# Hashed attention and SwiGLU on one core: two head pairs of batch 0 turned later, three casts of q on another engine, value means and weight loads at other slots

## The chip, the cores and the metric

The kernel runs on one core of a Trainium2 chip. The metric is the device time of one execution in microseconds, and lower is better. Three executions of the kernel before took 342.06, 342.91 and 343.15 us, so the median is 342.91 us.

## The reference

There are 4 batches with 8 heads each, 768 positions per head and 64 values per position. Attention is masked by a hash: a query sees a key only if the signs of their projections on 6 random directions agree. The result goes through an RMS norm and a SwiGLU block with 512 model columns and 1536 hidden columns.

```python
q_bits = (np.einsum('bhsd,dk->bhsk', q, proj) > 0).astype(np.int64)
k_bits = (np.einsum('bhsd,dk->bhsk', k, proj) > 0).astype(np.int64)
q_bucket = np.sum(q_bits * powers, axis=-1)
k_bucket = np.sum(k_bits * powers, axis=-1)
mask = q_bucket[:, :, :, None] == k_bucket[:, :, None, :]
scores = scale * np.matmul(q, k.transpose(0, 1, 3, 2))
scores = np.where(mask, scores, -1000000000.0)
scores = scores - np.max(scores, axis=-1, keepdims=True)
attn = np.exp(scores)
attn = attn / (np.sum(attn, axis=-1, keepdims=True) + 1e-09)
return np.matmul(attn, v).astype(np.float32)

rms = np.sqrt(np.mean(x * x, axis=-1, keepdims=True) + 1e-06)
xn = x / rms * rms_g
g = xn @ w_gate
silu = g * (1.0 / (1.0 + np.exp(-g)))
val = xn @ w_val
return (silu * val @ w_out).astype(np.float32)
```

## The kernel before

The work is cut into eight units `u`: four batches, each with two halves of 384 query rows. A unit has eight heads, and a head of a unit has three chunks of 256 keys. One chunk is one slot. `scores` makes two matmuls from the fp16 tile `QK` into `s_ps`, `probs` makes one exponential (L333) from it into `psb`, and `av` multiplies `psb` with the values `vl` into `o_ps`. The 6 signs of the hash are 6 more rows of `QK` (rows 64 to 69), so that the score matmul itself adds a large number where the buckets agree, and the exponential's bias takes it away. `cvb` holds a small multiple of the value means and is added to `o_ps` in `attn_out` (`otmp`, L360), then divided (`rcp`, `x`) and squared (`sq`) for the norm.

Heads come in pairs `hp`. A pair of batch 0 is brought into `QK` by these steps. `load_natural` loads q and k (tiles `qn`, `kn`), `load_v` the values (`vn`); all come from the queue of SyncE (SP) and take one of eight buffers of `lpool`, so a load waits for the last reader of its buffer. `turn_pe` turns one head on TensorE with three transposes into a PSUM bank (`t_ps`) and VectorE copies that into `qT` or `kT` (L150). `cast_pool` casts to fp16 into `QK` with two instructions on GpSimd (POOL), each for one half of the positions and both heads; a single such cast is `cast_part` (L164), which takes the engine as an argument. `hash_pair` makes 16 matmuls on `qT` and `kT` into two banks `d_ps` (L222), and `signs` turns these into `bits` on VectorE (L211). `send_pair` moves the bits into `QK` with four DMAs on SP (L261), in the order k and q of the first head, then k and q of the second; pair 1 moves one head with VectorE copies instead (L252). `v_prep` casts the values into `vl` (L290), and `v_mean` makes six matmuls (`m_ps`, L306) and writes `cvb` (L309). All these banks come from a pool of three.

The order is written out by hand. `at(w, s, f, ...)` puts a step into slot `24 * w + s`. In slot t the program first gives out `scores` of slot t+1, then `probs` of slot t, then the slot's steps, so each engine has its instructions in that order and keeps to it. Heads run as units 0 and 1 alternating for the first pair, then heads 2 to 7 of unit 0, then heads 2 to 7 of unit 1. So scores of batch 0's pair 1 are first made in slot 11 (for slot 12), those of pair 2 in slot 17 (for slot 18), and those of pair 3 in slot 23 (for slot 24). The last head of unit 0 has its `av` in slots 31 and 32, then follow its norm, `turn_x` in slot 37, and from slot 38 on the gate and value matmuls (`g_ps`, `v_ps`, L425) of unit 0, which need the weights `wg` and `wv`. These weights are loaded with a cast by the queue of POOL (`load_w`, L520), in halves of the hidden columns.

Batch 1's first two pairs are prepared in the same stretch: their loads stand in slots 8 and 17, their turns in slots 22 to 25 and 27 to 30. The norm's scale `rstd` is computed on POOL; the second weight halves stand behind it in POOL's order.

Of the kernel before, what the change touches and what calls it, by code (L numbers as in the profile page):

```python
# [33 lines left out]
def kernel(  # L34
# [12 lines left out]
    nc = tc.nc  # L47
# [485 lines left out]
    def at(w, s, f, *a):  # L533
        plan[NS * w + s].append(lambda: f(*a))
# [43 lines left out]
    at(0, 0, second_head)  # L578
    at(0, 1, cast_part, 0, 0, "q", 1)
    at(0, 1, v_prep, 0, 0)  # L580
    for hp, s0 in ((1, 2), (2, 5), (3, 11)):
        at(0, s0, new_pair, 0, hp)
        at(0, s0, turn_pe, 0, hp, 0, "k")
        at(0, s0 + 1, turn_pe, 0, hp, 1, "k")
        at(0, s0 + 1, cast_pool, 0, hp, "k")
        at(0, s0 + 2, turn_pe, 0, hp, 0, "q")
        at(0, s0 + 3, turn_pe, 0, hp, 1, "q")
        at(0, s0 + 3, cast_pool, 0, hp, "q")
        at(0, s0 + 4, hash_pair, 0, hp)
        if hp == 1:  # L590
            at(0, s0 + 5, send_pair, 0, hp, (1,))
            at(0, s0 + 5, move_head, 0, hp, 0)
        else:
            at(0, s0 + 5, send_pair, 0, hp)
# [4 lines left out]
    at(0, 8, v_prep, 0, 1, nc.vector)  # L599
    at(0, 13, v_prep, 0, 2, nc.vector)  # L600
    at(0, 19, v_prep, 0, 3, nc.vector)
    for hp, t in enumerate((4, 18, 24, 30)):
        at(0, t, v_mean, 0, hp, 2, range(6))
    for i, t in enumerate((20, 33)):
        cols = slice(i * DFF // 2, (i + 1) * DFF // 2)
        at(0, t, load_w, wg, moe_w_gate, 0, 4, cols)
        at(0, t + 3, load_w, wv, moe_w_val, 0, 4, cols)
        at(0, 39 + 3 * i, load_w, wo, moe_w_out, 6 * i, 6)
# [121 lines left out]
    def behind_norm(t):  # L730

        return t - t % NS + 7 if 2 <= t % NS < 7 else t

    for (b, hp), (load, kturns, qturns, _) in spots.items():
# [7 lines left out]
        t = behind_norm(qturns[-1] + 2)  # L742
# [66 lines left out]
```

## Time and profile before

| quantity | value |
|---|---|
| median of three executions | 342.91 us (342.06 to 343.15) |
| profiled execution, its own time | 340.8 us |
| its span, first to last instruction | 339.0 us |
| TensorE busy | 330.5 us, 97% |
| ScalarE busy, of it exponentials L333 | 224.6 us, 168.0 us |
| VectorE busy | 234.4 us |
| GpSimd busy | 151.2 us |
| granted TensorE clock, mean | 1.000 |
| first and 39th exponential start | 9.54 and 50.92 us |
| first gate matmul starts | 51.09 us |

The span is counted from the first to the last instruction, and 1.8 us of the execution's time lie around it. The list of costly groups is led by the exponentials (192 of 900 ns) and by the matmuls of scores, gate, value and projection. In the order of time, a row has the start in us, the length in us, the engine, the line, the operation, the tiles and how many instructions are merged; in brackets stands how long the engine was idle before it and what ended that. "SPq" rows are SyncE's DMA issues, and a row of several issues includes the time that the queue stood waiting between them.

### The profile page before, as it was taken

The page shows a single profiled execution, that of the slowest core. Times are in us where ns is not written, and L with a number is a line of the kernel's source. Part 1 is how long each engine was busy: PE and PEld are TensorE (multiplying, and loading weights), DVE is VectorE, ACT ScalarE, POOL GpSimd, SP SyncE. Part 2 cuts the span into 40 slices and gives each one's busy share as a digit, 9 for nine tenths or more (in the row PEclk, how much of TensorE's full clock was granted, in tenths as well). Part 3 has the DMA queues.
Part 4 walks back from the last instruction along what each step waited for, and adds up shares of the span by engine and source line. Part 5 has one row for each costly group of instructions (what it writes and reads, how often), then busy time and mean ns, then how long its engine had stood idle before and what let it go on. Part 6 is the DMA issues. An engine that isn't in the chain of part 4 may idle for free.

```text
span 339.0 us, 7797 instructions
## 1 busy us (share of the span) xinstructions
PE 330.5 (97%) x3004; PEld 197.4 (58%) x3004; DVE 234.4 (69%) x489; ACT 224.6 (66%) x325; POOL 151.2 (45%) x204
## 2 busy tenths in 40 slices
PE   7899899999999999999999999999999999999996
PEld 3565656655566556655656556555656656664554
DVE  3786696776879658884788658884776546674870
ACT  2878787676757767776677667776667767764322
POOL 3577848517463533747373523738281121112000
PEclk9999999999999999999999999999999999999999
DMA  7942989981809618070826118000200010001002
GB/s 243 316 144 22 262 135 209 221 154 36 190 19 164 118 65 169 8 141 6 163 76 96 51 65 167 9 1 7 95 3 3 2 62 34 0 2 64 32 0 93
DMA packets 79692, 30.92 MB, mean 91 GB/s; under 512 B 64988, under 2 KB 76712, under 8 KB 79656
## 3 DMA queue, kind: packets, MB, share of 16 engines
q1 hardware_dynamic: 75528, 25.45, 31.2%
q0 software_dynamic: 3680, 4.72, 8.4%
q8 instruction: 23, 0.38, 0.5%
q10 hardware_dynamic: 448, 0.27, 0.2%
q14 instruction: 13, 0.11, 0.1%
HBM read 28.32 MB, written 6.29 MB: 102 GB/s over the span
## 4 chain that ended last, share of the span: by engine, by line
PE 90%; DVE 4%; DMA 3%; ACT 2%; issue 1%; POOL 0%; DVEq 0%
PE v_ps L425 18%; PE g_ps L425 18%; PE y_ps L454 17%; PE s_ps L321 17%; PE o_ps L346 9%; PE d_ps L202 3%; DMA qn<-in_q_dram 3%; PE d_ps L222 2%; PE x_ps L408 2%; PE t_ps L148 2%; ACT psb L333 2%; PE z_ps L515 1%; PE y_ps L473 1%; DVE a L442 0%; PE m_ps L306 0%
## 5 line engine op out<-in xcount | busy, mean ns | idle before, releaser
L333 ACT ACTIVATE psb<-s_ps,ebias 128x768 f16<-128x768 f32 x192 | 168.0, 900 | 26.9 <-PE s_ps L321 25.9
L321 PE MATMUL s_ps<-QK 70*128 70x384 f16 x384 | 93.9, 326 | 1.8 <-ACT psb L333 1.1
L433 ACT ACTIVATE t<-g_ps 128x384 f32<-128x384 f32 x96 | 47.2, 491 | 56.1 <-PE g_ps L425 55.9
L425 PE MATMUL g_ps<-xnT,wg 128*128 128x384 f16 x384 | 82.5, 325 | 0.2
L425 PE MATMUL v_ps<-xnT,wv 128*128 128x384 f16 x384 | 81.7, 325 | 0.3 <-DVE a L442 0.2
L442 DVE SCALAR_TENSOR_TENSOR a<-t,g_ps 128x384 f32<-128x384 f32 x96 | 52.8, 550 | 28.2 <-ACT t L433 26.8
L454 PE MATMUL y_ps<-wo,ht 128*128 128x512 f16 x276 | 68.0, 378 | 0.0
L367 POOL TENSOR_TENSOR x<-otmp,rcp 128x384 f32<-128x384 f32 x31 | 25.7, 830 | 89.6 <-DVE rcp L365 89.3
L346 PEld LDWEIGHTS <-psb 128*128 128x128 f16 x1152 | 52.2, 97 | 15.8 <-issue 0.6
L443 DVE SCALAR_TENSOR_TENSOR ht<-a,v_ps 128x384 f16<-128x384 f32 x96 | 53.2, 554 | 11.7 <-PE v_ps L425 3.2
L346 PE MATMUL o_ps<-vl,psb 128*128 128x65 f16 x1152 | 56.3, 193 | 0.0
L321 PEld LDWEIGHTS <-QK 70*128 70x128 f16 x384 | 34.7, 98 | 35.5 <-issue 11.9
L425 PEld LDWEIGHTS <-wv 128*128 128x128 f16 x384 | 35.2, 97 | 22.6 <-issue 1.8
L425 PEld LDWEIGHTS <-wg 128*128 128x128 f16 x384 | 34.7, 97 | 21.2 <-DVE xnT L414 0.6
L454 PEld LDWEIGHTS <-ht 128*128 128x128 f16 x276 | 24.7, 97 | 22.7
L372 POOL TENSOR_TENSOR sq<-x 128x384 f32<-128x384 f32 x31 | 25.7, 828 | 2.4
L194 POOL CAST QK<-kT 64x768 f16<-64x768 f32 x20 | 16.4, 822 | 22.6 <-DVE kT L174 10.0
L466 ACT COPY ysb<-y_ps 128x512 f32<-128x512 f32 x23 | 13.5, 586 | 18.5 <-PE y_ps L454 18.5
L360 DVE TENSOR_TENSOR otmp<-o_ps,cvb 128x390 f32<-128x390 f32 x32 | 17.9, 559 | 10.3 <-PE o_ps L346 10.1
L194 POOL CAST QK<-qT 64x768 f16<-64x768 f32 x20 | 16.5, 827 | 18.4 <-DVE qT L181 17.0
L376 DVE TENSOR_REDUCE ssp<-sq 128x3 f32<-128x384 f32 x32 | 17.0, 530 | 10.0 <-POOL sq L372 10.0
L414 DVE TENSOR_TENSOR xnT<-x_ps,gcol 128x512 f16<-128x512 f16 x22 | 14.5, 685 | 5.8 <-PE x_ps L408 5.8
(70 smaller groups left out, 262.8 us busy)
## 6 DMA issues: line engine op xcount, KB each, us to landing
vn<-in_v_dram SPq DMA_DIRECT2D x16, 384.0 KB
out_dram<-ysb SPq DMA_DIRECT2D x23, 256.0 KB
qL<-in_q_dram SPq DMA_DIRECT2D x40, 96.0 KB
kL<-in_k_dram SPq DMA_DIRECT2D x40, 96.0 KB
kn<-in_k_dram SPq DMA_DIRECT2D x5, 384.0 KB
qn<-in_q_dram SPq DMA_DIRECT2D x5, 384.0 KB
wg<-in_moe_w_gate_dram POOLq DMA_DIRECT2D x2, 768.0 KB, 7.5
wv<-in_moe_w_val_dram POOLq DMA_DIRECT2D x2, 768.0 KB, 11.3
```

The source lines that it names most:

```text
L194: nc.gpsimd.tensor_copy(QK[b, 2 * hp + hh, "h"][0:64, o : o + S], src[64 * hh : 64 * hh + 64, :])
L321: nc.tensor.matmul(ps[:, j, 0:HALF], QK[b, h, "h"][0:KROWS, S + jt * 128 : S + (jt + 1) * 128], QK[b, h, "h"][0:KROWS, half * HALF : (half ...
L333: nc.scalar.activation(psb[u, h][:, 2 * ch : 2 * ch + 2, :], sps.pop((u, i))[:, :, 0:HALF], AF.Exp, bias=ebias, scale=ESCALE,)
L346: nc.tensor.matmul(o[:, c, hh, 0:65], psb[u, h][:, jt, c * 128 : (c + 1) * 128], vls[b % 2][:, h, 2 * (jt % 3) + jt // 3 if b in PARITY el ...
L360: nc.vector.tensor_add(tmp[:, :, :, 0:65], o[:, :, :, 0:65], cvb[b % 2][:, 2 * hp : 2 * hp + 2, 0:65].unsqueeze(1).to_broadcast([128, 3, 2 ...
L367: eng.tensor_mul(xd.rearrange("p c (h d) -> p c h d", h=2), tmp[:, :, :, 0:64], r.to_broadcast([128, 3, 2, 64]),)
L372: eng.tensor_mul(sq, xd, xd)
L425: nc.tensor.matmul(ps, w[:, kt, fs], xnT[u][:, kt, :], start=(kt == 0), stop=(kt == 3))
L433: nc.scalar.activation(t, fbank[u, ft, "g_ps"], AF.Tanh, scale=0.5)
L442: nc.vector.scalar_tensor_tensor(out=a, in0=t, scalar=1.0, in1=g, op0=ALU.add, op1=ALU.mult)
L443: nc.vector.scalar_tensor_tensor(out=ht[u][:, ft, :], in0=a, scalar=0.5, in1=vv, op0=ALU.mult, op1=ALU.mult)
L454: nc.tensor.matmul(y, ht[u][:, ft, c * 128 : (c + 1) * 128], wo[:, ft, :], start=(ft == 0), stop=(ft == NF - 1),)
```

## The change

Pairs 2 and 3 of batch 0 start their turns in slots 8 and 14, where they started in slots 5 and 11; casts, hash and sending of the bits keep their distance to that start, so pair 2's bits are sent in slot 13 and pair 3's in slot 19. For pairs 1, 2 and 3 the cast of q is split: its first half of the positions goes to VectorE, its second stays on POOL. Since pair 3's bits are now sent in slot 19, the loads of batch 1's pair 1, still in slot 17, stand ahead of them in SP's queue. The value means of pairs 1, 2 and 3 move from slots 18, 24 and 30 to slots 16, 21 and 31, and the weight halves of `wg` from slots 20 and 33 to 22 and 34; `wv` follows three slots behind each.

```diff
-    for hp, s0 in ((1, 2), (2, 5), (3, 11)):
+    for hp, s0 in ((1, 2), (2, 8), (3, 14)):
         at(0, s0, new_pair, 0, hp)
         at(0, s0, turn_pe, 0, hp, 0, "k")
         at(0, s0 + 1, turn_pe, 0, hp, 1, "k")
         at(0, s0 + 1, cast_pool, 0, hp, "k")
         at(0, s0 + 2, turn_pe, 0, hp, 0, "q")
         at(0, s0 + 3, turn_pe, 0, hp, 1, "q")
-        at(0, s0 + 3, cast_pool, 0, hp, "q")
+        at(0, s0 + 3, cast_part, 0, hp, "q", 0, 0, 2, nc.vector)
+        at(0, s0 + 3, cast_part, 0, hp, "q", 1)
         at(0, s0 + 4, hash_pair, 0, hp)
...
-    for hp, t in enumerate((4, 18, 24, 30)):
+    for hp, t in enumerate((4, 16, 21, 31)):
         at(0, t, v_mean, 0, hp, 2, range(6))
-    for i, t in enumerate((20, 33)):
+    for i, t in enumerate((22, 34)):
         cols = slice(i * DFF // 2, (i + 1) * DFF // 2)
         at(0, t, load_w, wg, moe_w_gate, 0, 4, cols)
         at(0, t + 3, load_w, wv, moe_w_val, 0, 4, cols)
```

## The prediction

> **What bounds the kernel now.** I read the page's first two parts, then busy time by stretch, then the chain of waits before 56 us, then ScalarE's, SyncE's and the other queues' order of time there.
>
> ```profile
> span 339.0 us, 7797 instructions
> PE 330.5 (97%) x3004; PEld 197.4 (58%) x3004; DVE 234.4 (69%) x489; ACT 224.6 (66%) x325; POOL 151.2 (45%) x204
> ...
> 35.00:40.00 5.00, 4.60 (x62) 3.07 (x60) 3.97 (x9) 3.82 (x6) 3.97 (x7) 1.00 1.12 276
> 40.00:45.00 5.00, 4.19 (x65) 2.97 (x65) 3.00 (x7) 3.93 (x5) 2.98 (x4) 1.00 1.16 243
> 60.00:80.00 20.00, 20.00 (x175) 11.72 (x174) 14.80 (x29) 13.08 (x19) 8.15 (x11) 1.00 0.91 167
> 160.00:280.00 120.00, 119.96 (x1101) 71.84 (x1100) 84.42 (x181) 84.72 (x121) 52.30 (x68) 1.00 0.24 57
> ```
>
> The columns behind each stretch are its length, then PE, PE loads, DVE, ACT, POOL, granted clock, DMA share, GB/s. From 60 us TensorE has no idle time; before 50 us it has. Slot 38, whose exponential starts at 50.92 us, brings the first gate matmuls. What brings slot 38 forward is won whole, what delays it is lost whole: all work of the full stretch is the same before and after.
>
> In the ramp, slot t holds TensorE's scores t+1, ScalarE's exponential t and the listed steps. ScalarE, with its idle time ahead of an exponential in brackets:
>
> ```profile
> 22.38 2.48 ACT L333 ACTIVATE psb<-s_ps,ebias 128x768 f16<-128x768 f32 x3 [1.55 <-PE s_ps L321]
> 28.47 8.48 ACT L333 ACTIVATE psb<-s_ps,ebias 128x768 f16<-128x768 f32 x10 [1.06 <-PE s_ps L321]
> 38.57 0.90 ACT L333 ACTIVATE psb<-s_ps,ebias 128x768 f16<-128x768 f32 x1 [0.63 <-PE s_ps L321]
> 39.82 1.89 ACT L333 ACTIVATE psb<-s_ps,ebias 128x768 f16<-128x768 f32 x2 [0.34 <-PE s_ps L321]
> 42.59 3.50 ACT L333 ACTIVATE psb<-s_ps,ebias 128x768 f16<-128x768 f32 x4 [0.88 <-PE s_ps L321]
> ```
>
> Counted from 9.54 us these begin with exponentials 11, 17, 28, 29 and 31. Ten in a row take 8.48 us, 0.85 each: ScalarE's own pace. The first two gaps are the hashes of pairs 2 and 3: TensorE stands in front of them until VectorE has copied the last turned q. The last two are these loads of batch 1's pair 1:
>
> ```profile
> 23.24 8.62 SPq L261 DMA_DIRECT2D QK<-bits  x8
> 31.91 0.45 SPq L94 DMA_DIRECT2D kn<-in_k_dram  x1
> 32.46 0.85 SPq L94 DMA_DIRECT2D qn<-in_q_dram  x1
> ...
> 32.46 8.89 DMA qn<-in_q_dram
> 41.35 0.04 issue
> ...
> 38.94 0.52 PE L148 MATMUL t_ps<-ident,kn 128*128 128x128 f32 x3 [0.40 <-DMA kn<-in_k_dram]
> 41.40 0.55 PE L148 MATMUL t_ps<-ident,qn 128*128 128x128 f32 x3 [0.69 <-DMA qn<-in_q_dram]
> ```
>
> SyncE gives the loads out only after the eight moves of bits, the last four of which wait for pair 3's signs; weights in flight stretch them to 7.0 and 8.9 us. TensorE stands still at 38.5 and 40.7 us.
>
> **The change part by part.** It removes no work: 12 transposes of pairs 2 and 3, three value means, all loads remain. Three casts go from POOL to DVE.
>
> *Pairs 2 and 3 three slots later.* VectorE sets this stretch, so I walk its new order by rows. Pair 1's signs start at 17.20 as now (its turns stay; its DVE cast, about 0.6, fits in the 0.76 us in which VectorE waits for that hash). Two signs 1.02, two moves of bits 1.25, one k copy 0.55, the value cast 0.56, otmp and rcp 0.75, one k and two q copies 1.65: pair 2's last q copy ends at 23.0. In the trace the exponential behind such a hash starts 1.36 after that copy's end (21.02 to 22.38, and 27.11 to 28.47). So exponential 14 starts at 24.4; now it is 22.38 + 3 x 0.84 = 24.9. TensorE's and POOL's shorter lists end earlier. Onward: the hash's matmuls end 0.92 after the copy (27.11 to 28.03), the new DVE cast lies in that gap; signs 1.0 end at 24.9; value cast 0.6, squares' sum 0.54, k copy 0.55, otmp and rcp 0.75, k and q copies 1.1, mean 0.29, q copy 0.55: pair 3's last q copy ends at 29.3, exponential 20 starts at 30.7, against 28.47 + 3 x 0.85 = 31.0. So the stall of a hash is not removed, it moves to slots 14 and 20; 0.3 us is won.
>
> *Bits closer to their use.* Pair 2's are wanted by scores 18, five slots behind its hash where there were eight; pair 3's by scores 24. Pair 3's signs ended at 29.05, and packets of the four moves ran at 30.3, 31.0, 31.7 and 32.3: k and q of the first head are there 2.3 after the signs. Pair 2: 24.9 + 2.3 = 27.2, and scores 18 are wanted at about 27.3 (exponential 16 ends at 24.4 + 3 x 0.85 = 26.95, and TensorE still has slot 16's transposes, product and mean). Pair 3: signs end at 29.3 + 0.92 + 1.0 = 31.2, bits 33.5; scores 24 are wanted when exponential 22 ends, 30.7 + 3 x 0.85 = 33.25. Exponential 24 at 33.5 + 0.33 + 0.3 for starting = 34.1 against 34.4 now. Bounds: 2.0 to 3.5 for the landing (first packets, and all four moves), so 0.3 better to 0.9 worse here.
>
> *Batch 1's pair 1 loads ahead of pair 3's bits.* By the changed program's order SyncE has pair 2's four moves (24.9 + 2.75 = 27.7, at the trace's 0.69 each), then the three loads, then pair 3's bits. The loads wait for buffers that a turn of slot 11, the value cast of slot 13 and a turn of slot 15 free, all before 27.9 us. They are given out by 29.1, some 4.2 us earlier. Pair 0's three loads, alone on the DMA engines, were given out from 19.91 to 21.31 and their traffic ended at 24.8; the same here gives 32.6, long before slots 27 to 30 turn them. Then exponentials 28 to 31, 4.02 us apart now, follow at 3 x 0.85 = 2.54: 1.48 won. The first gap, 0.63 before exponential 28, is the hash of batch 1's pair 0 and stays.
>
> *Value means.* Three groups of six matmuls, 0.35 each, same number. The one from slot 30 to 31 lies just ahead of the last attention product of batch 0; slot 31 then holds 0.33 + 0.35 + 0.27 = 0.95 against ScalarE's 0.875 there (3.50 / 4): 0.1 lost.
>
> *POOL and the weights.* POOL loses three casts of 0.83. It is not the bound: behind slot 14's rcp (27.3 by the walk) come x and sq 1.7, two k casts 1.71 and one q cast 0.83, ending at 31.6, before scores 24 are wanted. The cast's price on DVE: nearest row the value cast, 0.56 to 0.67. Even at 0.8 (POOL's own time) it lies in the 0.92 wait for the hash. The first half of wg now stands behind the x and sq of slot 20 (signs 31.2, value cast 0.6, sum 0.54, otmp and rcp 0.75: 33.1, then 0.85 twice): issue at 34.8 where it was 30.64; wv follows that issue (1.0), two casts (1.71) and gcol (0.23), at 37.9 where it was 34.36. Weight loads land in 7.2 to 13.7 us. wg by its 7.7 in that window: 42.5. wv by the median 11.3: 49.2; first needed at 51.74 - 1.6 = 50.1. I take nothing; bounds 0 and, by 13.7, 1.5. The second halves are given out behind rstd now (47.39, 48.25) and stay there.
>
> Two rules weigh against this. Row: where VectorE's SBUF casts or the second move of bits met POOL casts, the pair of POOL casts took 1.90 to 2.10 instead of 1.71 and that move took 0.885. The Trainium skill, SBUF — State Buffer, on the engine and DMA ports, says the two engines take one port pair as a lock for a whole instruction. By it each new DVE cast could first wait out a POOL cast, 0.83 + 0.56 = 1.4, which passes the 0.92 gap by 0.5. The rows show 0.2 to 0.5 of waiting, so less than a whole cast. The sum by the row is -1.6, by that rule at its worst -0.2 (rival B). Second, the page DMA: Bandwidth & Descriptors, Queues, rings and completion order, says a ring's descriptors are taken in order; pair 3's bits then stand behind 1.2 MB (rival C); no row here separates that from plain sharing.
>
> *Sum.* -0.3 - 1.48 + 0.1 = -1.7; I take -1.6 for small frictions. The norm chain from the last otmp (44.47) to the first gate (51.09) is a fixed 6.6 us and starts that much earlier. The profiled execution took 340.8 us (span 339.0 and 1.8 around it), 2.1 below the median of 342.91; the difference is carried to the median: 342.9 - 1.6 = 341.3.
>
> **Rivals.**
> A2. *The hashes stall less.* If VectorE's otmp and copies overlap as at 21.53 to 22.23, each walk is 0.4 shorter: 2.4 won, 340.5. For: rows overlap by 0.05 to 0.1. Against: seven to nine operations with nothing between them.
> B. *DVE casts wait for POOL.* At 15.98, 22.95 and 29.3 us a POOL cast is starting or running. Signs then come 0.4 (pair 1) and 0.5 (pair 2) later, all of which VectorE's walk hands on, and pair 3's bits another 0.5: 1.4 given back, 342.7, no change.
> C. *Pair 3's bits stand behind the loads: slower.* Place: scores 24. If the loads take the 8.9 us of the trace instead of 3.5, traffic ends near 37, bits with it, and TensorE waits 3.6 us at 33.4: 3.6 - 0.3 - 1.4 = 1.9 lost, 344.8. It is a loss from a landing of about 35.1 us. For: two slots lie between the last issue and the bits. Against: the 8.9 us had wg beside it, which now comes at 34.8.
> D. *wv late.* Landing at 51 (13.1 us after issue, wo's mean) instead of 49.2 gives back 0.9: 342.2.
>
> **How the numbers follow.** Forecast 0.52, A2 0.08, B 0.12, C 0.18, D 0.10. A difference of 0.3%, 1.0 us, is about what a measurement of this kernel can tell from no change. Faster by more: 0.47 of the forecast, all of A2, 0.03 of D: 0.58. Slower by more: 0.16 of C and 0.02 of B: 0.18. The rest 0.24. The likeliest case alone spans 340.7 to 342.2 (landing and frictions). The range runs from 340.2, which takes in A2, to 343.6, which takes in B, D and mild C; severe C, 0.13, and 0.05 below stay out.
>
> **What would show it.** SyncE's loads of batch 1's pair 1 at 27.5 to 29 and no DMA wait at transposes; exponential 14 near 24.4, 20 near 30.7, 24 near 34.1, 31 near 40.9; wg issued near 35; slot 38's exponential near 49.3. Wrong if scores 18 or 24 wait for a DMA by over 0.5, if casts of q on DVE exceed 0.9, or if the first v_ps waits for wv.

## The result, and the profile after

The changed kernel takes 339.37 us (median of 6, 338.75 to 340.08) against 342.02 us of the kernel before in the same measurements (6, 341.2 to 343.15): a ratio of 0.992, interval 0.9897 to 0.9944. It is faster, as forecast, but 339.37 us lies below the forecast range of 340.2 to 343.6. The profiled execution took 339.4 us; the forecast for it was 340.8 - 1.6 = 339.2 us. Executions of one kernel differ in the clock granted to TensorE: in the set of the repeat below, 18 of 24 executions of the kernel before had a mean of 0.998 or more and a median of 341.2 us while the other 6 took 342.57 to 346.24, and of the changed kernel 10 of 12 had it, at a median of 339.52, while the other 2 took 341.56 and 342.19.

The head of the changed kernel's page:

```profile
span 337.6 us, 7795 instructions
PE 329.3 (98%) x3004; PEld 198.3 (59%) x3004; DVE 235.8 (70%) x492; ACT 224.0 (66%) x325; POOL 149.2 (44%) x201
```

Its busy time by stretch, with the columns as before:

```profile
30.00:35.00 5.00, 3.82 (x58) 3.09 (x56) 3.31 (x9) 3.71 (x5) 4.25 (x5) 1.00 0.50 183
35.00:40.00 5.00, 5.00 (x70) 3.53 (x67) 4.03 (x10) 4.37 (x6) 4.53 (x7) 1.00 0.84 125
40.00:45.00 5.00, 5.00 (x78) 3.46 (x77) 4.24 (x10) 4.85 (x7) 3.30 (x5) 1.00 1.16 210
60.00:80.00 20.00, 20.00 (x170) 11.54 (x167) 14.97 (x29) 13.09 (x20) 8.03 (x12) 1.00 0.89 159
```

TensorE's idle time at 35 to 45 us is gone (4.60 and 4.19 busy before, 5.00 twice now); a hole at 30 to 35 us has grown (3.82 busy where it was 4.63). The full stretch is as it was. ScalarE's order of time shows the same, exponential by exponential:

```profile
10.09 0.90 ACT L333 ACTIVATE psb<-s_ps,ebias 128x768 f16<-128x768 f32 x1 [0.74 <-PE s_ps L321]
...
23.97 3.28 ACT L333 ACTIVATE psb<-s_ps,ebias 128x768 f16<-128x768 f32 x4 [0.42 <-PE s_ps L321]
27.90 1.77 ACT L333 ACTIVATE psb<-s_ps,ebias 128x768 f16<-128x768 f32 x2 [0.65 <-PE s_ps L321]
30.09 3.27 ACT L333 ACTIVATE psb<-s_ps,ebias 128x768 f16<-128x768 f32 x4 [0.42 <-PE s_ps L321]
34.56 2.56 ACT L333 ACTIVATE psb<-s_ps,ebias 128x768 f16<-128x768 f32 x3 [1.21 <-PE s_ps L321]
38.61 8.54 ACT L333 ACTIVATE psb<-s_ps,ebias 128x768 f16<-128x768 f32 x10 [0.63 <-PE s_ps L321]
49.50 0.92 ACT L333 ACTIVATE psb<-s_ps,ebias 128x768 f16<-128x768 f32 x1
```

These rows begin with exponentials 0, 14, 18, 20, 24, 28 and 38. The first one varies between 9.29 and 10.10 us from run to run, so I count every row from the first exponential of its own run. So counted, the changed kernel is ahead by 1.5 us at exponentials 14 and 20, by only 0.4 at 24, by 2.0 at 31 and by 1.97 at 38 (49.50 - 10.09 = 39.41 against 50.92 - 9.54 = 41.38). From slot 38 to the end both take 288.1 us. What eats 1.1 us at exponential 24 is in TensorE's and SyncE's rows:

```profile
27.53 0.39 SPq L94 DMA_DIRECT2D kn<-in_k_dram  x1
...
30.70 11.03 SPq L261 DMA_DIRECT2D QK<-bits  x8
...
33.98 0.48 PE L321 MATMUL s_ps<-QK 70*128 70x384 f16 x2 [1.06 <-DMA QK<-bits]
```

The loads are given out 4.4 us earlier (27.53 for 31.91; 4.9 counted from the first exponential), and no transpose waits for them any more. Pair 3's bits go out behind them, and scores 24 wait for those bits.

### The profile page after: what moved, and what is told of

Its sections match the earlier page's. It is cut to its first block, busy times and chain, and to the rows that moved or that the text cites. A ratio compares the mean times of both kernels' runs of the same rounds, so it can differ in the third digit from the quotient of the medians.

```text
span 337.6 us, 7795 instructions
## 1 busy us (share of the span) xinstructions
PE 329.3 (98%) x3004; PEld 198.3 (59%) x3004; DVE 235.8 (70%) x492; ACT 224.0 (66%) x325; POOL 149.2 (44%) x201
## 4 chain that ended last, share of the span: by engine, by line
PE 91%; DVE 4%; DMA 2%; ACT 1%; issue 1%; SPq 0%; DVEq 0%
PE v_ps L425 18%; PE g_ps L425 18%; PE s_ps L321 17%; PE y_ps L454 17%; PE o_ps L346 10%; PE d_ps L202 3%; PE t_ps L148 2%; PE x_ps L408 2%; PE d_ps L222 2%; DMA qL<-in_q_dram 1%; PE z_ps L515 1%; DVE bits L211 1%; PE y_ps L473 1%; DMA QK<-bits 1%; ACT psb L333 1%
## 5 line engine op out<-in xcount | busy, mean ns | idle before, releaser
L321 PEld LDWEIGHTS <-QK 70*128 70x128 f16 x384 | 34.5, 98 | 36.4 <-issue 11.0
```

Of the source, the lines that this page charges most:

```text
L321: nc.tensor.matmul(ps[:, j, 0:HALF], QK[b, h, "h"][0:KROWS, S + jt * 128 : S + (jt + 1) * 128], QK[b, h, "h"][0:KROWS, half * HALF : (half ...
```

## The experiments

All are timed against the kernel before in rounds. The "ramp" is the time from exponential 0 to exponential 38 in the run's ScalarE rows; it was 41.38 us before and 39.41 us in the changed kernel.

### The changed kernel again

No edit.

> The changed kernel once more, to size the gain with a narrower interval. Walk of both traces, each counted from its own first exponential: exponential 38 comes 1.97 us earlier, and nothing behind it changes. If that is all of the change, the ratio is 0.9942 (2.0 of 342). If part of the gain lies outside the profiled pair, it stays near 0.992.

Measured: 0.9942 (0.9914 to 0.9971), median 339.55 against 341.48 us, ramp 48.67 - 9.29 = 39.38 us. The 1.97 us of the ramp are what this set shows (341.48 - 339.55 = 1.93), and the first set's 0.992 agrees with it within its interval.

### Loads behind pair 3's bits again

```diff
-(1, (17, 27, 28, 29, 30, 29, 41, 32, 33, 43))
+(1, (20, 27, 28, 29, 30, 29, 41, 32, 33, 43))
```

> The changed kernel with batch 1's pair 1 loads put behind pair 3's bits again (slot 20). Theory (loads' wait worth 1.46, given back whole): scores of slot 24 no longer wait for bits as long, if the loads in flight delay these bits (second move landing 2.3 to 2.5 us after the signs instead of 3.2, 0.8 won there), but the turns of slots 27 and 29 wait for the loads again, 1.5 to 2.0 lost: about 340.5. Rival (loads are not what delays the bits): landing stays 3.1 to 3.2 after the signs, scores 24 wait 1.0 as now, and the time is about 341.

Measured: 0.9897 (0.9862 to 0.9933), 338.55 us, ramp 48.92 - 10.10 = 38.82 us. Both expectations fell. The bits land earlier, as the first one had it: scores 24 start 2.7 us after the signs' end (29.67 + 1.02 to 33.40) instead of 3.3 (30.67 to 33.98). (This trace puts the end of that wait down to an exponential; in the last version below, with the same order of moves and loads, it is the bits' DMA, at the same 2.7 us.) But no wait for the loads comes back, as SyncE's and ScalarE's order of time shows:

```profile
33.60 0.39 SPq L94 DMA_DIRECT2D kn<-in_k_dram  x1
...
38.03 8.55 ACT L333 ACTIVATE psb<-s_ps,ebias 128x768 f16<-128x768 f32 x10 [0.63 <-PE s_ps L321]
```

The loads go out at 33.60 us, later than the 31.91 of the kernel before, and still ten exponentials from number 28 on follow each other without a gap. So the loads' place in SyncE's queue is not what the change needs; here it costs 0.6 us. Something else keeps the loads fast.

### Loads ahead alone

```diff
 (kernel before)
-(1, (17, 27, 28, 29, 30, 29, 41, 32, 33, 43))
+(1, (15, 27, 28, 29, 30, 29, 41, 32, 33, 43))
```

> The kernel before with this one edit: batch 1's pair 1 loads in slot 15, so ahead of pair 3's bits, which are sent in slot 16. Theory: the gaps of 0.34 and 0.88 before exponentials 29 and 31 go, 1.2 to 1.5 won, 340.6; bits of pair 3 have seven slots until they are wanted and cost nothing. Rival (the gain is all from the later turns): no change, 342.

Measured: 0.9939 (0.9908 to 0.997), 340.04 us, ramp 50.24 - 9.80 = 40.44 us. In the kernel before the earlier loads do help, by 0.94 in the ramp: the gaps of 0.34 and 0.88 ahead of exponentials 29 and 31 are gone, the hash's gap ahead of 28 is 0.55, and a new one of 0.62 stands ahead of 27. What that one waits for was not settled.

### Later turns alone

```diff
 (kernel before)
-for hp, s0 in ((1, 2), (2, 5), (3, 11)):
+for hp, s0 in ((1, 2), (2, 8), (3, 14)):
-(1, (17, 27, 28, 29, 30, 29, 41, 32, 33, 43))
+(1, (20, 27, 28, 29, 30, 29, 41, 32, 33, 43))
```

> The kernel before with only the turns of pairs 2 and 3 in slots 8 and 14, casts on POOL, means and weights as before, and the loads in slot 20, so behind pair 3's bits as before. Theory: exponentials 14 to 23 come 1.0 to 1.5 earlier than before, the wait for pair 3's bits at slot 24 gives 1.0 of it back, and the loads come as late as before: 341.5 to 342. Rival (the later turns carry the change): 340.

Measured: 1.0162 (1.0108 to 1.0216), 347.97 us, ramp 57.83 - 10.09 = 47.74 us: slower by 6.4. Neither expectation had this. TensorE's order of time, with its waits in brackets:

```profile
38.98 0.48 PE L321 MATMUL s_ps<-QK 70*128 70x384 f16 x2 [2.57 <-DMA QK<-bits]
42.64 0.52 PE L148 MATMUL t_ps<-ident,kn 128*128 128x128 f32 x3 [1.66 <-DMA kn<-in_k_dram]
45.75 0.47 PE L148 MATMUL t_ps<-ident,qn 128*128 128x128 f32 x1 [1.33 <-DMA qn<-in_q_dram]
```

The stretch behind these waits, in the view of busy time by stretch (the third column from the end is the granted clock, the second the DMA engines' share):

```profile
44.40:51.60 7.20, 5.87 (x48) 4.40 (x47) 2.10 (x6) 3.38 (x5) 1.64 (x2) 0.53 0.84 154
```

The last moves of pair 3's bits, wanted by scores 27, were given out by 33.5 us, were wanted at 36.4 and landed only at 38.9, with wg given out at 32.12 and the DMA engines' share at 1.01 from 33.5 to 38.9 us. Then k and q loads are late too. After these waits the granted clock is 0.53 over 7.2 us, and scores take up to 0.85 us in it where they take 0.49 elsewhere. The difference to the version with the loads behind is the casts, the means, and the weights' slots; the next experiment takes the weights.

### Weights in their old slots

```diff
 (changed kernel)
-for i, t in enumerate((22, 34)):
+for i, t in enumerate((20, 33)):
```

> The changed kernel with the weight halves in their old slots 20 and 33, all else as changed. Theory A (the later weights are the part that keeps the DMA engines free for the bits): wg goes out near 32.0, 1.4 after the first of pair 3's bits, and the third and fourth move, wanted by scores 27 at about 36, land near 38 to 39: TensorE waits 2 to 3 us, 342. Theory B (my prediction: the weights' slot costs nothing either way): no DMA wait beyond the present 1.1 at scores 24, 339.5.

Measured: 1.001 (0.9974 to 1.0045), 342.28 us, ramp 52.01 - 9.83 = 42.18 us. The whole gain is gone, by this one edit. Theory A holds in its cause and was off in the place: it is the first two moves of the bits that wait. In the order of time of SyncE's queue, POOL and TensorE:

```profile
30.44 13.80 SPq L261 DMA_DIRECT2D QK<-bits  x8
31.67 1.00 POOL L520 DMA_DIRECT2D wg<-in_moe_w_gate_dram  x1
34.89 0.48 PE L321 MATMUL s_ps<-QK 70*128 70x384 f16 x2 [2.23 <-DMA QK<-bits]
```

The two stretches behind that wait, in the same columns:

```profile
34.90:36.40 1.50, 1.50 (x19) 1.31 (x20) 0.56 (x1) 0.93 (x2) 0.34 (x2) 1.00 1.11 193
36.40:39.80 3.40, 3.40 (x35) 1.89 (x32) 1.57 (x3) 2.35 (x3) 2.96 (x5) 0.51 1.14 207
```

The bits land 4.5 us after their signs (29.39 + 1.02 to 34.89) where the changed kernel has 3.3, and 1.5 us later the granted clock goes to about half for 3.4 us. The wait is 1.17 longer than the changed kernel's (2.23 against 1.06) and 3.4 us at about half clock cost 1.7: together 2.8, and the ramp is 2.77 longer.

### Later weights alone

```diff
 (kernel before)
-for i, t in enumerate((20, 33)):
+for i, t in enumerate((22, 34)):
```

> The kernel before with only the weight halves moved to slots 22 and 34; loads still behind pair 3's bits. Theory A: wg goes out at 34.4 instead of 30.64, so the loads given out at 31.9 to 33.9 have the DMA engines alone until about 35.8 and land by 37.5; the gaps of 0.34 and 0.88 ahead of exponentials 29 and 31 go and 1.2 to 1.5 are won: 340.1. Theory B (only the order in SyncE's queue decides when the loads land): no change, 341.5.

Measured: 0.9937 (0.9914 to 0.996), 339.92 us: theory A. For the trace the same kernel was run once more:

> The kernel before with only the weight halves in slots 22 and 34, again, for its trace (the first look at it fell into an execution with the clock at 0.66). Theory: wg goes out near 34.4, the three loads given out at 31.9 to 33.9 land before the transposes of slots 27 and 29 want them, exponentials 28 to 34 follow without the gaps of 0.34 and 0.88, and slot 38's exponential comes 1.3 to 1.5 earlier than before: 340. Rival: the loads still land late and the gain lies behind slot 38, in the weights themselves.

Measured: 0.9941 (0.9914 to 0.9968), 339.64 us, ramp 49.81 - 9.90 = 39.91 us, 1.47 shorter than before; from slot 38 to the end it is 288.1 us as ever, so the rival falls. The loads leave SyncE at the same place as in the kernel before, behind pair 3's bits, and are on time, as the order of time of ScalarE, SyncE's queue and POOL shows:

```profile
28.82 9.46 ACT L333 ACTIVATE psb<-s_ps,ebias 128x768 f16<-128x768 f32 x11 [1.05 <-PE s_ps L321]
38.92 6.05 ACT L333 ACTIVATE psb<-s_ps,ebias 128x768 f16<-128x768 f32 x7 [0.63 <-PE s_ps L321]
...
32.26 0.45 SPq L94 DMA_DIRECT2D kn<-in_k_dram  x1
34.70 1.00 POOL L520 DMA_DIRECT2D wg<-in_moe_w_gate_dram  x1
```

The gaps of 0.34 and 0.88 ahead of exponentials 29 and 31 are closed by giving the first weight halves out later, wg at 34.70 instead of 30.64 us and wv at 37.80 instead of 34.36, with the loads where they were. Which of the two mattered more is not separated.

### Both of them

```diff
 (kernel before)
-(1, (17, 27, 28, 29, 30, 29, 41, 32, 33, 43))
+(1, (15, 27, 28, 29, 30, 29, 41, 32, 33, 43))
-for i, t in enumerate((20, 33)):
+for i, t in enumerate((22, 34)):
```

> The kernel before with the loads of slot 17 in slot 15 and the weight halves in slots 22 and 34; turns, casts and means as before. Theory: both edits take away the same wait, so their gains do not add: 340.0, as each alone (0.9937 and 0.9939). Rival: each takes away another wait, and together they win 4 us: 338.

Measured: 0.9931 (0.9902 to 0.996), 339.74 us, ramp 49.47 - 9.55 = 39.92 us. The gains do not add; it is one wait, and either edit takes it away.

### Casts of q back on POOL

```diff
 (changed kernel)
-at(0, s0 + 3, cast_part, 0, hp, "q", 0, 0, 2, nc.vector)
-at(0, s0 + 3, cast_part, 0, hp, "q", 1)
+at(0, s0 + 3, cast_pool, 0, hp, "q")
```

> The changed kernel with all casts of q on POOL again. Theory: the DVE casts lie in VectorE's waits for the hash and POOL is not what is waited for, so the time stays at 339.5 within 0.4; POOL's wg goes out about 0.8 later. Rival: POOL's extra 0.83 per pair delays q of pair 3 past the moment scores 24 want it, or the product's x and sq, and the time is over 340.5.

Measured: 0.9914 (0.9888 to 0.994), 338.98 us, ramp 48.68 - 9.74 = 38.94 us. Not slower; the ramp is 0.47 shorter than the changed kernel's. The exponentials to number 23 stand where they stood; the wait for bits at scores 24 is 0.52 instead of 1.06. Loads and bits are given out at the same times from exponential 0 in both, and why the bits land earlier with the casts on POOL was not settled.

### Means in their old slots

```diff
 (changed kernel)
-for hp, t in enumerate((4, 16, 21, 31)):
+for hp, t in enumerate((4, 18, 24, 30)):
```

> The changed kernel with the value means in their old slots 18, 24 and 30. Theory: 0.35 of TensorE each, in slots with as little room, so within 0.3 of 339.5. Rival: the mean in slot 18, next to pair 3's hash, makes pair 3's bits later by up to 0.5 and the wait at scores 24 longer: 340.

Measured: 0.9952 (0.992 to 0.9983), 339.62 us, ramp 49.49 - 9.50 = 39.99 us. The time does not tell it from the changed kernel. The trace does: the gap ahead of exponential 20 is 0.77 instead of 0.42, and exponentials 24 to 27 take 3.77 us instead of 3.42. At exponential 28 this kernel is 0.57 behind the changed one, and it is still 0.58 behind at 38: 0.6 us of the ramp is the means' part. A gap of 0.23 ahead of exponential 35 is back too, but nothing of it reaches slot 38.

### Looking for a better version

The changed kernel with the loads in slot 20 and pair 3 turned from slot 13 on:

```diff
-for hp, s0 in ((1, 2), (2, 8), (3, 14)):
+for hp, s0 in ((1, 2), (2, 8), (3, 13)):
-(1, (17, 27, 28, 29, 30, 29, 41, 32, 33, 43))
+(1, (20, 27, 28, 29, 30, 29, 41, 32, 33, 43))
```

> The changed kernel with loads behind pair 3's bits (slot 20) and pair 3 turned from slot 13 on. Theory: bits of pair 3 are sent one slot earlier, the idle time of 0.61 ahead of exponential 24 in the version with loads behind the bits goes, and all else stays: 338.0. Rival: pair 3's hash meets VectorE's queue one slot earlier and TensorE waits the same 0.6 there instead: 338.5.

Measured: 0.9917 (0.989 to 0.9944), 339.03 us. No gain over the version with the loads behind alone. No trace shows where the slot went, so that stays open.

The changed kernel with the loads in slot 20 and the casts of q on POOL:

```diff
-at(0, s0 + 3, cast_part, 0, hp, "q", 0, 0, 2, nc.vector)
-at(0, s0 + 3, cast_part, 0, hp, "q", 1)
+at(0, s0 + 3, cast_pool, 0, hp, "q")
-(1, (17, 27, 28, 29, 30, 29, 41, 32, 33, 43))
+(1, (20, 27, 28, 29, 30, 29, 41, 32, 33, 43))
```

> The changed kernel with the loads behind pair 3's bits (slot 20) and the casts of q back on POOL, so only later turns, later weights and means. Theory: neither the casts nor the loads' order carries the gain once the weights come later: 338.5 to 339.0, no slower than the changed kernel. Rival: POOL then gives wg out late enough, or the loads land late enough, that a wait at slots 27 to 30 comes back: 340.

Measured: 0.9916 (0.9885 to 0.9946), 338.91 us, ramp 48.85 - 9.92 = 38.93 us. As expected: neither the casts nor the loads' order carries the gain. With the casts on POOL the loads' place is worth nothing (ramp 38.93 here, 38.94 with the loads ahead), so the 0.6 us that it costs in the changed kernel belongs to loads and casts together. From the version with later turns alone this one differs only by the new slots of weights and means: 338.91 against 347.97 us, a ramp shorter by 8.8 us. The means are worth 0.6 in the changed kernel; if that holds here, nearly all of the 8.8 is the weights' slots. Of the 2.45 us that it wins over the kernel before, later weights alone win 1.47; the other 0.98 belongs to turns and means, and no run separates these. The lowest ratio of all is the version with the loads behind (0.9897); its interval and those of the last two overlap, so no order among the three is claimed.

## Why the prediction was right or wrong

**The direction and the profiled execution: right.** A gain of 1.6 us was forecast, the ramp shows 1.97, and 339.4 us was measured for the profiled execution where 339.2 was forecast (its first exponential starts 0.55 us later than before, so it shows 1.4 of the 1.97). That this is so close is partly luck: two errors of about 1.1 us stood against each other in the sum, and its main cause was put down to the wrong edit. One of the signs of being wrong that the prediction named came: scores 24 wait 1.06 us for a DMA, over its limit of 0.5.

**The carry to the median: wrong, and it is the term that left the range.** The working added 2.1 us to go from the profiled execution to the median of the three executions shown, 342.91. Those three were a high sample: the six executions beside the first result, these three among them, have a median of 342.02, 24 beside the repeat 341.48, and those of the 24 at full clock 341.2, near the 340.8 of the profiled one. The clocks of the three are not on record, and some executions at full clock took over 342 us too, so why they were high is not shown. So 339.2, the profiled sum, was the better centre (339.37 and 339.55 were measured), and no bound of the range spoke of this.

**"Pairs 2 and 3 three slots later ... 0.3 us is won": mis-sized.** The form was right: exponentials 14 and 20 still start 1.36 us after the last q copy. The walk was too long. VectorE's rows of the changed kernel, from pair 1's signs to pair 2's cast, and behind them a POOL row of the kernel before:

```profile
17.45 1.02 DVE L211 TENSOR_SCALAR bits<-d_ps 128x384 uint16<-128x384 uint16 x2 [0.34 <-PE d_ps L222]
18.51 0.72 DVE L252 COPY QK<-bits 6x768 f16<-6x768 f16 x2
...
19.84 0.56 DVE L290 CAST vl<-vn 128x768 f16<-128x768 f32 x1
20.32 0.56 DVE L360 TENSOR_TENSOR otmp<-o_ps,cvb 128x390 f32<-128x390 f32 x1
...
21.02 0.52 DVE L150 COPY kT<-t_ps 128x384 f32<-128x384 f32 x1
21.45 1.16 DVE L150 COPY qT<-t_ps 128x384 f32<-128x384 f32 x2
22.65 0.75 DVE L164 CAST QK<-qT 64x768 f16<-64x768 f32 x1
...
18.75 1.90 POOL L164 CAST QK<-kT 64x768 f16<-64x768 f32 x2 [1.00 <-DVE kT L150]
```

Signs and moves begin 17.45 - 10.09 = 7.36 after exponential 0 (7.66 before). The two moves of bits take 0.72, not 1.25: in the kernel before POOL casts ran beside them from 18.75 us, and none runs at 18.51 to 19.23 now. Neighbouring rows overlap by 0.1. So the last q copy ends at 22.61, which is 12.52 after exponential 0 where the walk had 23.0 - 9.54 = 13.46. Of these 0.94 us the earlier start is 0.30, the moves 0.53 and the overlap about 0.1. From there to pair 3's last q copy (28.73) it is 6.12 where the walk had 6.3. So 1.5 us were won at exponential 20 and not 0.3. Rival A2 had the outcome, hashes that stall less, but by the overlap, which is the smallest part. ("12 transposes of pairs 2 and 3" is the number for one pair; nothing hangs on it.)

**"Bits closer to their use": mis-sized the other way.** The 2.3 us were read from packets. Scores 24 start 3.3 after the signs, within the bounds of 2.0 to 3.5; with the loads behind, 2.7. So the end of the packets is not yet the landing, and in the changed kernel the loads ahead add 0.6; with the casts on POOL they add nothing (2.8). The wait for the bits gives 1.1 of the 1.5 back at slot 24: exponential 24 is 0.4 ahead, where 0.3 was forecast. Rival C's place was right, its 3.6 us of wait was not reached; with the weights in their old slots it came nearer (2.23 us, and the gain gone), so C's remark that wg "now comes at 34.8" named the condition without a price.

**"Batch 1's pair 1 loads ahead ... 1.48 won": right number, wrong owner.** From exponential 28 to 31 the changed kernel takes 3 x 0.854 = 2.56 us, as forecast, against 4.02. But the later weights alone do it with the loads in their old place (1.47), and inside the changed kernel the loads' new place costs 0.6, with the casts on POOL nothing.

**"POOL and the weights ... I take nothing": the step that failed in its reading.** The times were right (wg 34.27 for 34.8, wv 37.54 for 37.9, the value weights in time). What they do to others was not asked: wg's slot was costed as a delay of wg, not as a freeing of the DMA engines for what SyncE gives out at the same time. With the weights back in their old slots the ramp is 2.77 us longer and the whole gain is gone.

**The casts and rival B.** The new DVE casts took 0.55, 0.75 and 0.55, and the hash's signs followed without delay: B did not come. POOL paid: its cast of q took 1.15 to 1.21 and its two k casts 2.03 and 2.06, where alone they take 0.83 and 1.71. VectorE paid too, at its value cast, which takes 0.56 alone:

```profile
24.48 0.90 DVE L290 CAST vl<-vn 128x768 f16<-128x768 f32 x1
...
22.93 2.03 POOL L164 CAST QK<-kT 64x768 f16<-64x768 f32 x2
24.91 1.15 POOL L164 CAST QK<-qT 64x768 f16<-64x768 f32 x1
```

The value cast starts while POOL's k casts have 0.48 us left, and takes 0.34 more; POOL's q cast starts while the value cast has 0.47 left, and takes 0.32 more. It is the same where the new casts meet POOL's (0.47 to 0.52 left, 0.32 to 0.38 more): whichever comes second grows by what is left of the other, less about 0.15, and the VectorE casts that came first keep their 0.55 us. The Trainium skill, SBUF — State Buffer, on the engine and DMA ports, says that VectorE and POOL take one port pair as a lock for a whole instruction; by the rows above this trace agrees. Rival B's price took a whole POOL cast for what was left of one, and here the new VectorE casts met at most 0.34 us of POOL work, which made one of them 0.75. With the casts on POOL the kernel is no slower.

**The mean in slot 31, "0.1 lost": not seen.** Ten exponentials from number 28 on run without a gap; with the means in their old slots the gap of 0.23 ahead of number 35 is back, though slot 38 comes no later for it. The 0.6 us that the means are worth show at the two that left slots 18 and 24, to which the working gave nothing.

## What to carry to other kernels

A long DMA that nobody waits for has a price: ask of each issue what else is in flight when its traffic runs, and move the large transfer that can wait before reordering the small ones that can't. Read the end of a transfer from who waits for it, not from its packets. And where the executions of a kernel differ by more than the effect, make the sum against the profiled execution, and do not add its distance from a median of three.

## What the runs showed of the hardware that was not expected

A move of 9 KB, given out behind a weight load on POOL's queue (wg at 32.12) and just ahead of three loads on its own queue, landed about 5.4 us after its issue (issued by 33.5, landed at 38.9 us), where the two moves of the run with the loads behind let scores 24 start 2.7 us after the end of the signs that they carry.

A wait of TensorE of 2.23 us was followed, 1.5 us later, by 3.4 us at about half the granted clock; waits of 2.57 and 1.66 us were followed by 7.2 us at 0.53, which hold a third wait of 1.33. The changed kernel's wait of 1.06 left the clock at 1.00 in its profile. One such stretch of 3.4 us at half clock is 1.7 us in 340, a mean clock of 0.995. Of the twelve executions of the version with the weights in their old slots eight have a mean clock of 0.994 or 0.995 and two have 1.000, so the stretch does not come every time. That the same waits cause the lower clocks of other versions is argued from this number, and no profile shows it.
